# Attention scores on smaller tiles of the TensorE array: 32 queries by 96 keys in place of 64 by 128, with one kept PSUM tile, an earlier memset and a new written-out order

## The chip, the cores and the metric

The kernel runs on one core of one Trainium2 chip. The metric is the device time of one execution in microseconds (us), as the median of the runs. Beside it there is one profiled execution, with a record of each instruction; its span is the time from its first to its last instruction. The engines are called PE (TensorE: matrix products), DVE (VectorE), ACT (ScalarE), POOL (GpSimd) and SP (SyncE, which here only issues DMAs).

## The reference

Three layers follow one another, in float32. The first is attention over a sliding window of 64 positions; the second mixes each position with the one before it and runs a gated two-layer network; the third gates with a causal convolution of five taps.

```python
batch, n_heads, seq, head_dim = 4, 8, 576, 64        # attention
scores = scale * np.matmul(q, k.transpose(0, 1, 3, 2))
rel = pos[:, None] - pos[None, :]
mask = (rel >= 0) & (rel < 64)
scores = np.where(mask, scores, -1000000000.0)
attn = exp(scores - max);  attn = attn / (sum + 1e-09)
x = attn @ v                                          # -> (4, 576, 512)

xk = mu_k * x + (1.0 - mu_k) * x_prev                 # second layer
xr = mu_r * x + (1.0 - mu_r) * x_prev
k = np.maximum(xk @ w_k, 0.0)                         # 512 -> 1024
v = k * k @ w_v                                       # 1024 -> 512
x = sigmoid(xr @ w_r) * v

gate = sigmoid(sum of 5 taps of x)                    # third layer
out = gate * (x @ w_val) @ w_out
```

The weights come in as float64 and are put together from two 32-bit words on the chip.

## The kernel before

The 4 x 576 positions are cut into five blocks t: one of 256 and four of 512. Attention works on units u = (block t, pair of heads hp), four units to a block, 20 in all. A query sees the 63 keys before it and its own, so a unit cuts its positions into chunks of 64 queries, and a chunk meets 128 keys. Chunks sit in PSUM by twos: an even chunk on partitions 0 to 63, an odd one on 64 to 127, one PSUM bank for each of the two heads.

Each unit goes through a chain of steps: `ldqk` and `ldv` (DMAs that load q, k and v), `qk` (PE: the scores, line 425), `mask` and `edge` (DVE and POOL: scale the scores and take the minimum with a mask tile `cap`), `top` (DVE: row maximum), `exp` (ACT, line 469), `eps`, `rec`, `norm` (DVE: divide by the sum), `tp0` and `tp` (PE: transposes, line 487), `pt` (ACT or DVE: copy out of PSUM), `pv` (PE: times v, line 499) and `x` (copy out). In the units of blocks 0 and 1 (`BY_PE`) PE itself writes the mask: before the scores it multiplies an identity with the tile `low`, in bfloat16 (lines 417 and 421), and the scores are added onto that. The scores are float32; one such product of the program is two weight loads and two matrix passes in the trace, so that a unit of eight chunks and two heads has 32 records on PE.

Block 0 has its own PSUM pool of two score tiles (`p0`). From block 1 on each unit asks the pool `pq`, which has one buffer, for a new tile, which is free when the step that reads the scores (`exp` or `mask`) of the unit before is done.

The matrix products of the second layer are `h` (w_k), `r` (w_r) and `v` (w_v), 512 positions wide from block 1 on (line 590), and those of the third layer `val` and `out` (lines 859 and 965). They run on all 128 x 128 cells of the array; the scores run on 64 x 64 tiles of it, `pv` on 128 x 64.

The order of every step on every engine is fixed by a table, `SLOT`, which gives each step its place and, with a letter, its engine where there is a choice (`a` ACT, `v` DVE, `p` POOL). A small planner, `Plan`, walks through the steps in that order and emits them; it also holds a cost for each, and where its own clock shows PE free for longer than `WAIT`, the function `fill` puts in products of a zeroed 128 x 128 tile, `warm`, whose results nobody reads ("idle products", line 1144). It stops doing that once the first unit of block 1 has its scores. DMAs are issued by SP in the order of the table.

At the start POOL makes the mask (`cap`), then the identity (`ident`), and then zeroes `warm` (line 319); DVE derives `low` and `one` from the first two.

Of the kernel before, what the change touches and what calls it, by code (L numbers as in the profile page):

```python
# [8 lines left out]
F32 = mybir.dt.float32  # L9
# [11 lines left out]
P = 128  # L21
W = 64
NT = B * S
# [5 lines left out]
TB = 512  # L29
# [143 lines left out]
class Plan:  # L173
# [5 lines left out]
    WAIT, PASS = 700, 600  # L179
# [57 lines left out]
def tile_kernel(ctx, tc, qkh, vh, mu, conv, w_k, w_v, w_r, w_val, w_out, out):  # L237
# [55 lines left out]
    op = plan.op  # L293
# [906 lines left out]
```

## Time and profile before

| | before |
|---|---|
| median of 3 runs | 427.52 us (427.39 to 428.42) |
| the profiled execution's own time | 427.77 us |
| its span | 425.7 us |
| outside the span | 2.07 us |
| busy: PE, DVE, ACT, POOL | 97%, 82%, 62%, 6% of the span |
| mean granted clock of TensorE | 0.990 of 2.4 GHz |
| moved by DMA | 77.61 MB, mean 182 GB/s |

The table is of one execution, on the one core. Busy shares are means over stages with different limits, and the end of a matrix pass is modelled in the profile, so that passes that run side by side on several tiles overlap in it.

### The profile page before, as it was taken

How to read it: one execution, taken by the hardware profiler on the slowest of the kernel's cores; microseconds unless marked ns; L12 is line 12 of the kernel's file. 1: busy time of each engine (PE TensorE's matmuls, PEld its weight loads, DVE VectorE, ACT ScalarE, POOL GpSimd, SP SyncE). 2: the span in 40 equal slices, each digit the busy share in tenths (PEclk: the TensorE clock that was granted, in tenths of full speed). 3: DMA queues.
4: the chain of work that ended last, by engine and by line, in shares of the span. 5: the costliest groups of instructions: out<-in, count | busy, mean ns of one | idle time of the engine just before them, and what ended most of it. 6: DMA issues, size and time to landing. Idle time of an engine off the chain costs nothing.

```text
span 425.7 us, 7996 instructions
## 1 busy us (share of the span) xinstructions
PE 413.1 (97%) x3160; PEld 355.4 (83%) x3160; DVE 347.1 (82%) x506; ACT 264.0 (62%) x596; POOL 25.8 (6%) x66
## 2 busy tenths in 40 slices
PE   5799999999999999999999999999999999999996
PEld 4578888888888888888888888888888999999996
DVE  3889979989898786867597987697667799999970
ACT  4989998668869535867325776165331565668631
POOL 1101101010021000000000000000010000001000
PEclk9889999999999999999999999999999999999999
DMA  6999850553233444034039254177999940417623
GB/s 203 398 417 397 287 216 2 166 151 109 88 105 104 142 134 155 27 93 161 0 143 341 92 183 162 51 260 286 347 407 384 351 141 31 168 28 182 154 111 113
DMA packets 24709, 77.61 MB, mean 182 GB/s; under 512 B 2528, under 2 KB 3296, under 8 KB 22624
## 3 DMA queue, kind: packets, MB, share of 16 engines
q1 hardware_dynamic: 23088, 66.88, 44.5%
q0 software_dynamic: 1440, 10.22, 7.6%
q8 instruction: 25, 0.41, 0.4%
q14 instruction: 12, 0.10, 0.1%
q10 hardware_dynamic: 144, 0.00, 0.0%
HBM read 53.90 MB, written 20.84 MB: 176 GB/s over the span
## 4 chain that ended last, share of the span: by engine, by line
PE 80%; DVE 13%; ACT 2%; DMA 2%; issue 1%; POOL 0%; SPq 0%; ACTq 0%; POOLq 0%
PE h L590 21%; PE v L590 21%; PE r L590 10%; PE at L499 4%; PE at L487 4%; PE qk L425 4%; PE v L613 3%; PE out L965 3%; PE val0m L859 2%; DVE gq L757 2%; PE out2m L859 2%; DMA s<-w_v 2%; DVE x L757 2%; PE h L613 2%; PE r L613 2%; DVE xt L747 2%
## 5 line engine op out<-in xcount | busy, mean ns | idle before, releaser
L590 PE MATMUL h<-x,wk 128*128 128x512 f32 x384 | 91.4, 393 | 0.0
L590 PEld LDWEIGHTS h<-x,wk 128*128 128x128 f32 x384 | 71.2, 188 | 14.6
L590 PE MATMUL v<-sh,wv 128*128 128x512 f32 x256 | 81.7, 392 | 0.0
L590 PEld LDWEIGHTS v<-sh,wv 128*128 128x128 f32 x256 | 48.0, 188 | 9.9
L590 PE MATMUL v<-sl,wv 128*128 128x512 f32 x128 | 49.8, 389 | 0.0
L590 PE MATMUL r<-x,wr 128*128 128x512 f32 x192 | 45.8, 391 | 0.0
L469 ACT ACTIVATE s<-s,m 128x128 f32<-128x128 f32 x96 | 37.4, 396 | 13.1 <-DVE m L458 13.1
L790 DVE SCALAR_TENSOR_TENSOR early<-early,wc 128x576 f32<-128x576 f32 x48 | 38.3, 815 | 5.9 <-ACT early L788 5.3
L590 PEld LDWEIGHTS r<-x,wr 128*128 128x128 f32 x192 | 35.7, 188 | 7.3
L590 PEld LDWEIGHTS v<-sl,wv 128*128 128x128 f32 x128 | 24.1, 188 | 4.8
L670 DVE TENSOR_TENSOR sl<-rk,sh 128x1024 fp32r<-128x1024 f32 x16 | 19.6, 1222 | 8.6 <-ACT rk L668 8.5
L487 PE MATMUL at<-ident,s 128*128 128x128 f32 x144 | 23.9, 287 | 2.1 <-ACT xT L506 1.4
L499 PEld LDWEIGHTS at<-pt,vt 128*64 128x64 f32 x576 | 19.0, 140 | 7.7 <-issue 4.1
L550 DVE SCALAR_TENSOR_TENSOR xm<-xT,omu,xm 128x512 f32<-128x512 f32 x32 | 22.2, 748 | 3.1 <-POOL xT L556 1.6
L487 PEld LDWEIGHTS at<-ident,s 128*128 128x128 f32 x144 | 16.7, 142 | 8.0 <-ACT xT L506 2.3
L499 PE MATMUL at<-pt,vt 128*64 128x64 f32 x576 | 21.9, 228 | 1.2 <-DVE pt L493 1.2
L479 DVE TENSOR_TENSOR s<-s,m 128x1024 f32<-128x1024 f32 (+1 forms) x20 | 22.3, 1114 | 0.2
L425 PE MATMUL qk<-qk 64*64 64x128 f32 x576 | 22.1, 290 | 0.0
L640 ACT ACTIVATE rk<-h 128x512 f32<-128x512 f32 (+1 forms) x30 | 15.4, 535 | 10.2 <-PE h L590 9.2
L794 ACT ACTIVATE early<-early 128x1152 f32<-128x1152 f32 x6 | 7.0, 1170 | 21.9 <-DVE early L790 21.9
L573 DVE TENSOR_TENSOR x<-xm,x 128x1024 fp32r<-128x1024 f32 x16 | 19.2, 1219 | 1.6 <-ACT x L570 1.5
L469 ACT ACTIVATE s<-qk,m 128x128 f32<-128x128 f32 x48 | 16.9, 384 | 4.9 <-DVE m L461 4.9
(178 smaller groups left out, 845.8 us busy)
## 6 DMA issues: line engine op xcount, KB each, us to landing
qk<-qk SPq DMA_DIRECT2D x16, 544.0 KB, 5.6
vt<-vh SPq DMA_DIRECT2D x16, 512.0 KB, 4.8
xb<-x2d SPq DMA_DIRECT2D x4, 1152.0 KB, 7.1
out_t<-st SPq DMA_DIRECT2D x15, 288.0 KB, 2.4
x2d<-sgs SPq DMA_DIRECT2D x16, 256.0 KB, 4.9
w_out<-w SPq DMA_DIRECT2D x8, 512.0 KB, 2.9
w_val<-w SPq DMA_DIRECT2D x8, 448.0 KB, 3.1
wk<-w_val POOLq DMA_DIRECT2D x2, 1792.0 KB, 12.0
```

Source lines behind the costliest of these rows:

```text
L425: PE.matmul(a["ps"][heads[c % 2], h, c // 2 * P:c // 2 * P + P], lhsT=a["q"][heads[h], c * W:(c + 1) * W], rhs=a["k"][heads[h], c * W:c * ...
L469: ACT.activation(out=s, in_=scores()[:, c // n2, c % n2, :] if by_pe else s, func=AF.Exp, scale=D ** -0.5 if by_pe else 1.0, bias=l(0)[:, ...
L479: lambda: V.tensor_tensor(out=a["s"], in0=a["s"], in1=l(1).unsqueeze(2).to_broadcast(sq), op=ALU.mult))
L487: PE.transpose(a["tp", h][:, c * P:(c + 1) * P], a["s"][:, h * n2 + c, :], ident)
L499: PE.matmul(a["o"][heads[h], c * W:(c + 1) * W], lhsT=a["v"][:, c, heads[h]], rhs=a["pt"][:, h, c * W:(c + 1) * W], start=True, stop=True)
L550: V.scalar_tensor_tensor(out=m, in0=xT[:, f, :n], scalar=omu[:, c:c + 1], in1=m, op0=ALU.mult, op1=ALU.add)
L573: lambda E: E.tensor_tensor(out=dst(1), in0=src(), in1=f32(dst(0)), op=ALU.subtract))
L590: PE.matmul(ps, lhsT=a, rhs=b[:, kt, :], start=(kt == 0 and i == 0), stop=(kt == nk - 1 and i == 2))
L613: PE.matmul(Ps[key][:, :n], lhsT=ws(kt), rhs=x()[:, kt, :], start=kt == 0, stop=kt == nk - 1)
L670: lambda E: E.tensor_tensor(out=Ss[t][1][:, f, :n], in0=rk(), in1=f32(Ss[t][0][:, f, :n]), op=ALU.subtract))
L757: lambda E: E.tensor_tensor(out=lo(), in0=src(), in1=f32(hi()), op=ALU.subtract))
L790: V.scalar_tensor_tensor(out=o, in0=x, scalar=c, in1=o, op0=ALU.mult, op1=ALU.add)
```

## The change

The diff has four parts.

1. The scores: a chunk of 64 queries becomes two of 32, and each meets 96 keys (63 before its first query and its own 32, rounded up to whole halves of a chunk). Four such chunks stand beside each other on partitions 0, 32, 64 and 96, and with two heads the products are spread over eight tiles of 64 x 32 cells in place of four of 64 x 64. There are twice as many products, each 96 columns wide in place of 128. The 32 columns of each row that are no longer written hold what the tile held before, and the mask covers them.
2. The PSUM tile: from block 1 on all units write into one tile that is kept (`Q["scores"]`), the same one that the idle products write.
3. The start: the memset of `warm` is called ahead of `masks`, which now depends on it, and the planner may fill from 900 on its clock and reckons 430 for an idle product, where it had 1100 and 600.
4. The table `SLOT` and the planner's cost of `qk`. Nearly every number of the table differs; a line is shown.

```diff
 SLOT = {
-    'qk': '16 18 32 27 39 78 110 135 173 196 241 298 329 346 369 413 438 472 499 522',
+    'qk': '17 18 32 26 39 75 111 134 188 226 286 314 332 356 380 421 448 468 499 532',
...
+HW = W // 2
...
-    WAIT, PASS = 700, 600
+    WAIT, PASS, WARM = 700, 430, 900
...
-                self.fill(t, int((t - max(free.get("pe", 0), 1100) - 250) // self.PASS))
+                self.fill(t, int((t - max(free.get("pe", 0), self.WARM) - 250) // self.PASS))
...
+    warm = sgs[:, 0, :P]
+    op("warm", "pool", 110, [], lambda: G.memset(warm, 0.0))
+
     def masks():
...
-    op("cap", "pool", 1300, [], masks)
+    op("cap", "pool", 1300, ["warm"], masks)
...
         def qk():
-            a["ps"] = (pq if t else p0).tile([P, 2, TB], F32, tag="qk" if t else "p0", name=f"qk{u}")
+            a["ps"] = Q["scores"] if t else p0.tile([P, 2, TB], F32, tag="p0", name=f"qk{u}")
...
-            for c in range(nc_):
+            for c in range(2 * nc_):
+                rows = slice(c % 4 * HW, c % 4 * HW + HW)
                 for h in (0, 1):
-                    PE.matmul(a["ps"][heads[c % 2], h, c // 2 * P:c // 2 * P + P],
-                              lhsT=a["q"][heads[h], c * W:(c + 1) * W],
-                              rhs=a["k"][heads[h], c * W:c * W + P], start=not by_pe, stop=True,
+                    o = c // 4 * P + c % 2 * HW
+                    PE.matmul(a["ps"][rows, h, o:o + W + HW], lhsT=a["q"][heads[h], c * HW:(c + 1) * HW],
+                              rhs=a["k"][heads[h], c * HW:c * HW + W + HW], start=not by_pe, stop=True,
                               skip_group_check=by_pe)
-        op(("qk", u), "pe", 1034 * nc_ // 8 + ...
+        op(("qk", u), "pe", 822 * nc_ // 8 + ...
...
     def first_idle():
-        idle["ps"] = pq.tile([P, 2, TB], F32, tag="qk", name="idle")
+        idle["ps"] = Q["scores"] = pq.tile([P, 2, TB], F32, tag="qk", name="scores")
```

On POOL, at the very start of the program, this stood before (`cap` is the mask, `sgs` the tile whose first part is `warm`):

```order
L304 AFFINE_SELECT cap<-cap 64x128
L306 AFFINE_SELECT cap<-cap 64x128
masks.py:197 MEMSET ident 128x128
masks.py:199 AFFINE_SELECT ident<-ident 128x128
L319 MEMSET sgs 128x128
L297 MEMSET xT 128x4
```

This stands there after the change:

```order
L300 MEMSET sgs 128x128
masks.py:197 MEMSET ident 128x128
masks.py:199 ISA
masks.py:199 AFFINE_SELECT ident<-ident 128x128
L307 AFFINE_SELECT cap<-cap 64x128
L309 AFFINE_SELECT cap<-cap 64x128
```

The memset that the idle products wait for went from last but one to first, and the identity ahead of the mask.

On PE the program begins with the idle products and the first unit's mask and scores. Before:

```order
L1144 MATMUL idle<-sgs 128x128 x4
L417 LDWEIGHTS one
L417 MATMUL qk_159<-low,one 64x256
...
L417 MATMUL qk_159<-low,one 64x256
L425 MATMUL qk_159<-qk_122 64x128 x8
```

After:

```order
L1146 MATMUL scores<-sgs 128x128 x6
L418 LDWEIGHTS one
L418 MATMUL qk_161<-low,one 64x256
...
L418 MATMUL qk_161<-low,one 64x256
L428 MATMUL qk_161<-qk_123 32x96 x16
```

Six idle products stand there in place of four, and the unit's eight score products have become sixteen of 32 queries by 96 keys; the mask's own products keep their shape of 64 rows.

On SP, which issues the DMAs, the last pieces of w_v (line 355, 128x2048) stood between the loads of q, k and v for later units like this:

```order
L355 DMA words<-w_v 128x2048
L398 DMA qk_588<-qk 128x1088
L398 DMA qk_596<-qk 128x1088
L404 DMA vt_600<-vh 128x1024
L355 DMA words<-w_v 128x2048
L404 DMA vt_657<-vh 128x1024
L398 DMA qk_694<-qk 128x1088
L355 DMA x_118<-w_v 128x2048
L404 DMA vt_753<-vh 128x1024
L355 DMA s_119<-w_v 128x2048
```

After the change:

```order
L356 DMA words<-w_v 128x2048
L399 DMA qk_631<-qk 128x1088
L356 DMA words<-w_v 128x2048
L324 DMA cw<-conv 128x40
L405 DMA vt_720<-vh 128x1024
L356 DMA x_118<-w_v 128x2048
L399 DMA qk_732<-qk 128x1088
L356 DMA s_119<-w_v 128x2048
```

Between the first and the last piece of w_v there are now three loads of q, k and v where there were six.

## Rows read from the trace of the kernel before

**Rows 1.** Busy time of each engine by stretch, with instruction counts, granted clock and DMA.

```profile
core 0: us, PE busy (x) PEld busy (x) DVE busy (x) ACT busy (x) POOL busy (x), PEclk, DMA share, GB/s
5.00:10.00 5.00, 4.04 (x72) 3.33 (x71) 2.39 (x7) 2.28 (x13) 0.00 (x0) 1.00 0.61 179
15.00:20.00 5.00, 2.78 (x34) 1.80 (x38) 4.00 (x10) 4.88 (x22) 0.73 (x1) 0.77 1.03 390
20.00:25.00 5.00, 5.00 (x57) 4.08 (x50) 4.79 (x10) 3.43 (x8) 0.00 (x0) 0.55 1.03 419
25.00:60.00 35.00, 35.00 (x441) 29.34 (x439) 31.32 (x43) 34.05 (x104) 4.39 (x8) 1.00 0.90 340
70.00:164.00 94.00, 94.00 (x935) 77.42 (x935) 84.04 (x114) 66.12 (x195) 8.15 (x23) 1.00 0.36 113
328.00:421.00 93.00, 91.69 (x680) 90.59 (x679) 80.77 (x116) 54.50 (x84) 3.88 (x7) 1.00 0.47 146
```

**Rows 2.** Score passes (line 425) by short stretch: in brackets, passes under way in it.

```profile
153.71:153.74 0.03, 0.02 (x4) 1.00 0.00 0
153.74:153.87 0.13, 0.13 (x4) 1.00 0.00 0
153.87:153.90 0.03, 0.03 (x8) 1.00 0.00 0
153.98:154.01 0.03, 0.03 (x12) 1.00 0.00 0
```

**Rows 3.** Chain that ended last, around that unit: start, length, what.

```profile
152.71 1.08 PE at L499 x32
153.79 1.03 PE qk L425 x32
```

**Rows 4.** The score passes as a group: count, busy us, mean ns, idle before.

```profile
L425 PE MATMUL qk<-qk 64*64 64x128 f32 x576 | 22.1, 290 | 0.0
```

**Rows 5.** PE in order of time, a unit whose mask PE writes.

```profile
35.29 0.41 PE L417 MATMUL qk<-low,one 64*64 64x512 bf16 x4
35.53 0.27 PE L425 MATMUL qk<-qk 64*64 64x128 f32 x2
```

**Rows 6.** The same chain as in Rows 3, its first 20 us.

```profile
3.05 0.15 POOL sgs L319
...
3.25 2.08 PE idle L1144 x8
...
7.72 0.99 ACT s L469 x5
...
18.60 0.69 PE at L487 x2
```

**Rows 7.** SP, POOL and DVE at the start, in order of time.

```profile
0.74 1.80 SPq L398 DMA_DIRECT2D qk<-qk  x4
...
1.07 0.29 POOL L304 TENSOR_SCALAR_AFFINE_SELECT cap<-cap 64x128 f32<-64x128 f32 x1 [0.63 <-DVE cap L300]
...
2.48 0.20 POOL masks.py:197 MEMSET ident<- 128x128 f32 x1
...
3.08 0.23 DVE L315 CAST one<-ident 128x128 bf16<-128x128 f32 x1 [0.32 <-POOL ident masks.py:199]
```

**Rows 8.** The tile `qk`, first 12 us: its DMAs from issue to landing.

```profile
DMA to landing us min/median/max: 3.0/3.8/5.9
```

**Rows 9.** The same chain as in Rows 3, from 50 us to 61 us.

```profile
50.31 8.22 DMA s<-w_v
...
58.55 0.70 DVE s L340
...
60.44 0.66 PE at L487 x4
```

**Rows 10.** Waits of PE: its line, whom it waited for, us, times, longest.

```profile
PE val3m L859 <- DVE early L900: 0.7, 1, 0.7
PE out2m L859 <- ACT x L754: 0.6, 1, 0.6
```

More of the change, by code (lines that the diff above doesn't have):

```diff
@@ L316, in tile_kernel @@
     op("low", "dve", 700, ["cap", "ident"], lows)
-    warm = sgs[:, 0, :P]
-    op("warm", "pool", 110, [], lambda: G.memset(warm, 0.0))
     op("table", "act", 100, ["warm"], lambda: ACT.activation(out=sgs[:, 1, :1], in_=warm[:, :1], func=AF.Exp), table="exp")
@@ L422, in qk @@
                                           rhs=low[heads[h], P:], start=False, stop=True, skip_group_check=True)
-            for c in range(nc_):
+            for c in range(2 * nc_):
+                rows = slice(c % 4 * HW, c % 4 * HW + HW)
                 for h in (0, 1):
-                    PE.matmul(a["ps"][heads[c % 2], h, c // 2 * P:c // 2 * P + P],
-                              lhsT=a["q"][heads[h], c * W:(c + 1) * W],
-                              rhs=a["k"][heads[h], c * W:c * W + P], start=not by_pe, stop=True,
+                    o = c // 4 * P + c % 2 * HW
+                    PE.matmul(a["ps"][rows, h, o:o + W + HW], lhsT=a["q"][heads[h], c * HW:(c + 1) * HW],
+                              rhs=a["k"][heads[h], c * HW:c * HW + W + HW], start=not by_pe, stop=True,
                               skip_group_check=by_pe)
-        op(("qk", u), "pe", 1034 * nc_ // 8 + (208 if t == 0 else 241) * by_pe, [("ldqk", u), *(["low"] if by_pe else []), *([] if t else ["idle"])], qk,
+        op(("qk", u), "pe", 822 * nc_ // 8 + (208 if t == 0 else 241) * by_pe, [("ldqk", u), *(["low"] if by_pe else []), *([] if t else ["idle"])], qk,
            ring=("pq" if t else "p0", ("exp" if by_pe else "mask", u)))
```

247 rows, old and new, of the table SLOT are left out of this document.

## The prediction

> **What bounds the kernel now.** I read the busy times by stretch first [rows 1]. From 25 us on PE is busy all the time: 35.00 us of 35, later 94.00 of 94, and 91.69 of 93 in the last stage. A busy PE need not be a fast one, so I looked at how the passes follow each other, and then at the chain that ended last, which lies almost wholly on PE from 19 us on. Time that PE saves after 25 us is therefore time saved at the end, as long as what PE needs also comes earlier. ACT leaves it little room in 25 to 60 us: it is busy for 34.05 of 35 us [rows 1]. Before 19 us PE waits for others: the chain runs from a POOL memset over idle products to the first scores, and then along ACT's exponentials, which begin at 7.72, until PE takes over at 18.60 [rows 6].
>
> The scores themselves are bound by their tiles. In one unit four passes are under way within the first 0.03 us, none joins them until 153.87, then four more come within 0.03 us, and again four from 153.98 on [rows 2]. Four tiles work side by side, all four are refilled at once, and a steady round takes 153.98 - 153.87 = 0.11 us: 1.03 us for a unit [rows 3] is 8 rounds (32 passes on 4 tiles) of 0.11 = 0.88, and a rest of 0.15. The rest is a longer first round (153.87 - 153.71 = 0.16 for 0.11) and the changes of the array's shape on the way in and out. No score pass waited for anything [rows 4].
>
> **The scores of blocks 2 to 4.** Removed are 32 passes on four tiles, added 64 on eight: again 8 rounds, each over 96 columns in place of 128. I scale the round with its columns: 0.11 x 96/128 = 0.083. A unit saves 8 x 0.027 = 0.22 us and takes 0.81, if the rest of 0.15 stays. Twelve units of blocks 2 to 4 lie in the stretches where PE never pauses [rows 1]: **-2.6 us**. No row shows 64x32 tiles, so this has bounds: nothing saved if the rest grows by what the rounds lose, and the loss in the first rival. The weight loads double in number, but each has half the columns and they run beside the passes as now. The kept PSUM tile costs nothing: a unit had to wait for the reader of the unit before it already, since the pool had one buffer, and that wait is covered by the `pv` and h, r, v products between two units [rows 4]. Without that cover PE would stand for the reader's time.
>
> **The scores of blocks 0 and 1.** Here the mask's passes come first, on 64x64 tiles. Now the scores follow 0.24 us after the mask's start, while a 512-column pass of the mask still shows as under way [rows 5]: the shape stays. After the change it changes between the two, eight times. The price lies between 0 and the whole rest of 0.15 us; I take 0.10, the part of it that is not the longer first round. The four units of block 1 then save 0.22 - 0.10 each, 0.5 together, and since ACT has only 0.95 us to spare there I count **-0.3 us** (bounds -0.9 and 0). The four half units of block 0 save 0.11 and pay 0.10. The Trainium skill (TensorEngine Tiling (Array Packing), Key Properties) says that a change of tiling mode, as against a change of tile, drains the engine; by it nothing near -0.9 can come of this term, and with the whole 0.15 for a drain it would be 4 x 0.07 = -0.3.
>
> **The start.** The idle products began at 3.25, right behind the memset at 3.05 [rows 6]. POOL could take up its own work at about 1 us: the first mask step at 1.07 had waited for DVE [rows 7]. With the memset in front I put the first idle product at 1.2. Four of them, 8 passes, took 2.08 us [rows 6], 0.26 a pass; six take 3.1, so that the mask's passes can begin at 4.3 and not at 5.33. Two other things must be there: q and k, issued at 0.74 and landing 3.0 us later, at 3.7 [rows 7, 8]; and `low` and `one`, for which POOL now works through memset (0.15), identity (2.48 to 3.05: 0.57) and mask (1.07 to 2.48: 1.41) from 1.0 to 3.1, and DVE another half microsecond, to some 3.7 [rows 6, 7]. So the first scores and ACT's exponentials come 1.0 us earlier, and what follows to 19 us hangs on ACT: **-1.0 us**. Bounds: 0, if the DMAs decide (their share is 1.03 from 15 to 25 us [rows 1]); -2.1, the memset's whole lead. In 5 to 10 us the DMA share was 0.61, partly since the next loads wait for the first scores, so loads can move up too.
>
> **The new order.** PE waited 1.3 us in the last stage (93.00 - 91.69 [rows 1]), nearly all of it twice [rows 10]. Another order can remove that or add as much: -1.3 to +1.3, and I take **0**. The places where PE changes its shape are the same but for one or two, by the order, 0.1 us each.
>
> **The sum.** -2.6 - 0.3 - 1.0 = -3.9: a span of 421.8 after 425.7, with the 2.07 us outside it 423.9. The profiled execution took 427.77, 0.25 above the median of 427.52, so the median to expect is **423.6 us**.
>
> **Rivals.**
>
> *PE can't start passes fast enough (slower).* A pass begins on average every 0.11/4 = 0.0275 us, and `pv`, on two tiles, is no faster: 32 passes in 1.08 us [rows 3]. If this is what PE can issue and not what the tiles take, 64 passes need 1.76 us and a unit 1.91, 0.88 more than now; with 16 full and 4 half units, 18 x 0.88 = 15.8, less 1.0 at the start: 442. The change loses in the scores as soon as a round of eight takes over 0.11, a start each 0.014 us. Against it: four passes begin within 0.03 us and then none for 0.13 [rows 2]; PE waits for tiles. But nowhere do more than four begin at once. I give it 0.12. The Trainium skill (TensorE: Matmul & The Clock Gate, section "Wait — 56ns, not 53.3ns?") states that start-to-start never drops below about 25 ns however small the product; by that a unit would take 64 x 0.025 + 0.15 = 1.75 and the kernel 439.5 (18 x 0.72 less 1.0). The rows speak against the rule as it stands, with four starts in 30 ns.
>
> *The clock no longer falls.* It was at 0.77 on average from 15 to 20 us and 0.55 from 20 to 25 [rows 1], that is at 1.2 GHz from about 17.7 to 24.5, after a stretch in which PE was busy for 2.78 us of 5. The same 5.0 busy us of 20 to 25 at full clock need 2.75: 2.2 us less, 421.4. More idle products (six and four for four and two in the order) speak for it; that they end in both kernels with block 1's first unit, long before 15 us, against it: 0.12.
>
> *The DMAs hold the start's gain back.* The last piece of w_v, issued at 50.31, landed at 58.55; DVE waited for it, and PE's transposes at 60.44 for DVE [rows 9]. If it lands no earlier, the 1.3 us gained before it are lost there: 424.9. Three loads fewer stand ahead of it now, against this: 0.12.
>
> *The scores gain nothing.* The rest grows by 0.22 with eight tiles; only the start is left: 426.5. 0.07.
>
> *The new order stalls.* It would need 3.9 us of new waits to eat the gain, three times those of the last stage [rows 10]; 427.5 to 430: 0.05.
>
> **How the numbers follow.** The forecast has the rest, 0.52, with a range of its own of 422.4 to 425.0. About 0.3% (1.3 us) is what a measurement of this kernel can tell from no change: faster is below 426.2, slower above 428.8. Faster: 0.52 + 0.12 + 0.12 = 0.76. The fourth rival and half of the fifth are no change: 0.09. The first and the other half are slower: 0.15. From 421.0 to 427.0 leaves out the first rival, most of the fifth and the edge of the second, 0.2.
>
> **What would show it.** A unit's 64 passes in 0.81 us on the chain, eight starts within some 0.05 us and a round of 0.08; passes at an even spacing of 25 ns or more would show the first rival. In blocks 0 and 1 a gap of about 0.1 us between mask and scores. The first exponential near 6.7 us. PE without a pause from 24 us on; the clock in 15 to 25 us; the landing of the last w_v before 58 us. I am wrong if a unit takes over 1 us, or if PE waits more than 1.3 us in the last stage.

## The result, and the profile after

The changed kernel is slower: 431.19 us median of 8 runs (430.0 to 433.84), against 427.63 us for the kernel before on the same chip (8 runs), a ratio of 1.0084 [1.0058, 1.0109]. The forecast was 423.6. The profiled execution took 432.7 us, with a span of 430.9 in place of 425.7.

First the view by stretch, which answers to [rows 1]: busy time of each engine with instruction counts, granted clock, DMA share.

```profile
core 0: us, PE busy (x) PEld busy (x) DVE busy (x) ACT busy (x) POOL busy (x), PEclk, DMA share, GB/s
15.00:20.00 5.00, 4.39 (x92) 3.00 (x94) 4.08 (x11) 4.90 (x20) 0.58 (x1) 0.54 1.00 399
20.00:25.00 5.00, 5.00 (x46) 4.04 (x47) 4.69 (x7) 3.53 (x19) 0.00 (x0) 0.77 1.03 419
25.00:60.00 35.00, 35.00 (x505) 29.78 (x504) 33.65 (x44) 34.17 (x85) 1.76 (x6) 1.00 0.87 330
70.00:164.00 94.00, 94.00 (x1287) 77.16 (x1286) 80.75 (x110) 69.93 (x201) 4.35 (x22) 1.00 0.38 121
320.00:330.00 10.00, 4.15 (x19) 3.19 (x17) 9.93 (x16) 3.07 (x4) 0.11 (x1) 0.97 0.32 124
330.00:340.00 10.00, 8.84 (x49) 8.85 (x50) 6.56 (x10) 1.30 (x2) 0.43 (x1) 0.69 1.00 352
```

Up to 320 us PE is as full as before. Then it is busy for 4.15 us of 10, and afterwards its clock is granted at 0.69 on average. The waits of PE (whom it waited for, us, times, longest) show one new entry for the last stage, where [rows 10] had nothing over 0.7:

```profile
PE val0m L861 <- DVE x L759: 7.0, 1, 7.0
...
PE val3m L861 <- DVE x L759: 0.3, 1, 0.3
```

`val0m` is the third layer's first product. Its group in the view by lines (count, ns of one as min/median/max, first and last start) gives the start of that layer; first after, then before:

```profile
L861 PE MATMUL val0m<-x,wk x84: 290/295/608, 323.9 to 346.1; 128*128 128x288 f32 x84
```

```profile
L859 PE MATMUL val0m<-x,wk x84: 292/295/302, 327.9 to 340.6; 128*128 128x288 f32 x84
```

So the changed kernel was 4.0 us ahead when the third layer began. From there to the end it took 430.9 - 323.9 = 107.0 us in place of 425.7 - 327.9 = 97.8. Of these 9.2 us the wait is 7.0, and the halved clock behind it makes up about the rest: one product takes up to 608 ns, and on the chain 59 passes take 10.41 us where 60 took 7.99 before, 2.4 more. That piece of the chain before:

```profile
328.09 7.99 PE val0m L859 x60
```

The chain after tells where the 7 us come from (start, length, what):

```profile
299.29 0.37 SPq L798
299.66 0.05 issue
299.88 19.01 DMA xb<-x2d
...
319.01 0.76 DVE xt L749
...
331.16 10.41 PE val0m L861 x59
```

The load of `xb`, the x of the third layer, is under way for 19.01 us. DVE then works through the last taps and the preparation of x until 331, ahead of PE. The timeline of POOL and SP's queue shows which other loads went out then:

```profile
290.79 1.27 POOL L1117 DMA_DIRECT2D wk<-w_val  x2 [90.66 <-PE h L592]
302.33 0.53 POOL L1120 DMA_DIRECT2D wr<-w_out  x1 [9.50 <-PE r L592]
302.85 1.07 POOL L1120 DMA_DIRECT2D wol<-w_out  x2
303.89 0.57 POOL L1120 DMA_DIRECT2D wr<-w_out  x1
```

```profile
295.25 0.37 SPq L779 DMA_DIRECT2D early<-x2d  x1
299.29 0.37 SPq L798 DMA_DIRECT2D gd<-early  x1
299.88 0.62 SPq L724 DMA_DIRECT2D xb<-x2d  x1
300.55 1.24 SPq L808 DMA_DIRECT2D gate<-gd  x1
```

And the same before, first on POOL, then the load of `xb` on SP's queue:

```profile
297.81 0.71 POOL L1115 DMA_DIRECT2D wk<-w_val  x1 [2.67 <-PE h L590]
302.57 0.55 POOL L1118 DMA_DIRECT2D wol<-w_out  x1 [4.05 <-DVE sl L670]
309.12 1.06 POOL L1118 DMA_DIRECT2D wr<-w_out  x2 [6.00 <-PE r L590]
310.17 0.55 POOL L1115 DMA_DIRECT2D wk<-w_val  x1
```

```profile
294.82 0.62 SPq L722 DMA_DIRECT2D xb<-x2d  x1
```

The DMA page gives 1792 KB for each `wk` load and 1024 KB for each of the four others, 7.7 MB together; at the 361 to 408 GB/s that the stretch from 300 to 320 us moves, that is about 20 us of all DMA engines, an estimate. Before, one `wk` went out at 297.81 and the other at 310.17, and `xb` stood ahead of both (issued at 294.82, 5.9 us to land). Now both go out at 290.79 and 291.49, ahead of everything that the third layer's start needs. They don't delay it alone: by the profile both had landed by 304.6 us (7.6 and 13.1 us after their issue), and `xb` was under way for another 14 us, beside the four loads of w_out that went out behind it.

The scores (chain, one unit, to compare with [rows 3]) did get shorter, by less than forecast (the chain runs through 55 of the unit's 64 passes):

```profile
149.93 0.93 PE scores L428 x55
```

### The profile page after: what moved, and what is told of

Read it like the earlier page. It is cut to its first block, busy times and chain, and to the rows that moved or that the text cites. A ratio compares the mean times of both kernels' runs of the same rounds, so it can differ in the third digit from the quotient of the medians.

```text
span 430.9 us, 9154 instructions
## 1 busy us (share of the span) xinstructions
PE 415.3 (96%) x3744; PEld 356.5 (83%) x3744; DVE 355.4 (82%) x524; ACT 253.5 (59%) x579; POOL 19.2 (4%) x67
## 4 chain that ended last, share of the span: by engine, by line
PE 72%; DVE 19%; DMA 6%; issue 1%; ACT 1%; SPq 0%; ACTq 0%; POOL 0%; DVEq 0%; POOLq 0%
PE h L592 18%; PE v L592 15%; PE r L592 8%; DMA xb<-x2d 4%; PE at L501 4%; PE at L489 4%; PE scores L428 4%; DVE x L759 4%; PE v L615 3%; PE h L615 3%; PE out L967 3%; PE val0m L861 2%; PE out2m L861 2%; DVE early L792 2%; DVE gq L759 2%; DVE xt L749 2%
## 5 line engine op out<-in xcount | busy, mean ns | idle before, releaser
L592 PE MATMUL v<-sh,wv 128*128 128x512 f32 x256 | 82.7, 394 | 0.0
L792 DVE SCALAR_TENSOR_TENSOR early<-early,wc 128x576 f32<-128x576 f32 x48 | 38.6, 813 | 11.3 <-ACT early L790 11.1
L642 ACT ACTIVATE rk<-h 128x512 f32<-128x512 f32 (+1 forms) x25 | 12.8, 541 | 13.6 <-PE h L592 8.7
L861 PE MATMUL val0m<-x,wk 128*128 128x288 f32 x84 | 14.1, 333 | 7.0 <-DVE x L759 7.0
L756 ACT ACTIVATE x<-xt 128x576 fp32r<-128x576 f32 x15 | 10.1, 681 | 18.1 <-issue 11.5
L861 PEld LDWEIGHTS val0m<-x,wk 128*128 128x128 f32 x84 | 13.6, 224 | 7.4 <-DVE x L759 7.3
```

The source lines that it names most:

```text
L592: PE.matmul(ps, lhsT=a, rhs=b[:, kt, :], start=(kt == 0 and i == 0), stop=(kt == nk - 1 and i == 2))
L792: V.scalar_tensor_tensor(out=o, in0=x, scalar=c, in1=o, op0=ALU.mult, op1=ALU.add)
L861: PE.matmul(z[bank][:, j, :HS], lhsT=lhs, rhs=rhs, start=new and kt == 0 and e == 0, stop=kt == 1 and e == 2, skip_group_check=not new)
```

## Experiments

All ratios are to the kernel before on the same chip; us of change are the ratio less 1, times 427.5.

| kernel | median us | ratio [95%] | change |
|---|---|---|---|
| e1: new scores only | 425.92 | 0.9973 [0.9958, 0.9988] | -1.2 |
| e4: new start only | 425.81 | 0.9967 [0.9950, 0.9984] | -1.4 |
| e8: both, old order | 425.81 | 0.9958 [0.9935, 0.9981] | -1.8 |
| e2: changed kernel, old scores | 434.98 | 1.0183 [1.0158, 1.0209] | +7.8 |
| e3: changed, `xb` load ahead | 433.06 | 1.0123 [1.0092, 1.0154] | +5.3 |
| e5: changed, w_val loads later | 426.72 | 0.9959 [0.9941, 0.9977] | -1.8 |
| e6: e5 and e3 | 425.99 | 0.9947 [0.9919, 0.9975] | -2.3 |
| e11: before, w_val loads together | 434.58 | 1.0185 [1.0166, 1.0205] | +7.9 |
| e9: changed, third layer's old order | 424.17 | 0.9930 [0.9909, 0.9951] | -3.0 |
| e10: e9 with old scores | 425.48 | 0.9964 [0.9948, 0.9980] | -1.5 |

**The parts apart (e1, e4, e2, e8).** e1 is the kernel before with the new score function and the kept tile alone; e4 has only the start:

```diff
-    'cap': '4',
+    'cap': '9',
-    'warm': '10',
+    'warm': '2',
-    WAIT, PASS = 700, 600
+    WAIT, PASS, WARM = 700, 430, 900
-    op("cap", "pool", 1300, [], masks)
+    op("cap", "pool", 1300, ["warm"], masks)
```

e2 is the changed kernel with the old score function, e8 the sum of e1 and e4. What was expected of e1:

> The kernel before with the scores alone changed (32 queries by 96 keys on eight tiles, the kept PSUM tile); start and order are those of before. In the profile of the changed kernel a unit of scores in blocks 2 to 4 took 0.93 us where it took 1.03, and a unit of block 1 with its mask 1.30 where it took 1.27. If that is all, 12 x -0.10 + 4 x 0.03 = -1.1 us: 426.5. Theory 'the order is to blame': 426 to 427. Rival 'the scores themselves lose time somewhere': 428 or more.

Of e4:

> The kernel before with the start alone changed: memset first, then identity and mask, six and four idle products in place of four and two; scores and order of before. In the changed kernel the third unit of block 1 began its mask at 26.92 and not 28.89, 2.0 us earlier. Theory 'the start's gain reaches the end': 425.5 to 426. Rival 'the last piece of w_v, landing at 58.55, holds it back': 427 to 427.5, with a longer wait of PE at 60 us.

Of e2:

> The changed kernel with the scores of before (64 by 128 on four tiles, a new PSUM tile for each unit); its start and its order stay. Theory 'the order is to blame': PE comes to the third layer 1.1 us later and waits there for the same late data, 6 us in place of 7, so the time stays near 431 (430 to 433). Rival 'the scores themselves lose': back to 427 or below.

Of e8:

> The kernel before with its order, plus the new start and the new scores with the kept tile. Theory: the two parts add up: -1.4 for the scores and -1.5 for the start as each alone gave, 424.4 us (423.9 to 425.0), and then the new order alone is worth about +6.8 us. Rival (the parts are held back by the same DMA, the last pieces of w_v, or by ACT's exponentials): no better than either alone, 425.8 us.

Each part alone gains, and of these kernels and the changed one only the two with the new order lose: e2, with the old scores, is even slower than the changed kernel and than the 430 to 433 expected. PE waits 9.4 us for `x` there, and `xb` is under way for 21.35 us. So neither the scores nor the start cause the loss. e8 doesn't tell whether the two gains add up: its median is where the rival had it, but its interval reaches from -0.8 to -2.8 us and holds the sum of -2.6 too. In e8's profile, its slowest execution, one transfer of w_r is under way for 9.82 us on the chain in the first 20 us; the runs of one kernel here differ by 1 to 6 us.

**The load of xb (e3).** The first theory was that `xb` is late because it stands behind the gate's store on SP's queue:

```diff
-    'ldx': '893 943 958 1015',
+    'ldx': '877 943 958 1015',
```

> The changed kernel with one number of its table altered: the load of the third layer's first batch (step ldx 0) moves ahead of the last-but-one gate's load and store on SP, behind the weight stores. Theory 'that load is late since it stands behind a store that waits for DVE and ACT': it is issued near 291 and not 299.9, lands by 300 and not 318.9, PE's wait of 7.0 us ahead of the third layer and the slow clock after it (2.3 us) go: 422 to 423. Rival 'DVE's backlog ahead of the third layer makes the data late in any case': the wait stays over 4 us, 428 or more. Rival 'the transfer is slow, since it shares the DMA engines with the other loads': issue earlier, landing still after 312.

The theory fell. `xb` now landed 14 us earlier, and PE still waited 6.7 us; on the chain another transfer of the same time had taken its place:

```profile
298.49 16.21 DMA gd<-early
...
314.81 0.79 ACT early L790
```

Of the two, the one that stands second on SP's queue is the one that lands late: in the changed kernel the store, issued at 299.29, landed in 7.5 us and `xb` behind it in 19.01. DVE takes the taps of the early gate (L792) ahead of x's preparation (L749 to L759), and stands until the store's buffer is free.

**The loads of w_val (e5, e6).** The next theory: the two `wk` loads fill the DMA engines.

```diff
-    'wv2': '870 872',
+    'wv2': '899 901',
```

> The changed kernel, with the two large loads of w_val moved on POOL's queue behind the first load of w_r (issued after about 301 us and not at 290.79 and 291.49). Theory: the 7 us wait of PE at the start of the last stage comes from these two loads, which fill the DMA engines while the x of the gate's early taps, its store and its reload stand in line. Then xb lands by about 306 us in place of 318.9, the wait is under 1 us, the clock does not fall at 330 us, and the time is 422 to 424 us. Rival (DVE's queue of taps and x preparation is late by itself, or the loads of w_r and w_out do the same): the wait stays above 5 us and the time at 428 us or more. A smaller loss is possible if w_val now lands after 324 us and PE waits for it instead.

> The changed kernel with both edits: the two loads of w_val later, and the load of xb ahead of the gate's store. Theory (full DMA engines): 421.5 to 423.5 us, no wait above 1 us at the start of the last stage, xb landing by about 301 us; little or no better than the later loads alone, since xb is then no longer last. Rival (DVE's queue or the other loads): 428 us or more, as the xb load moved by itself gave.

This line alone takes back 5.3 us (1.0084 to 0.9959). Two lines of POOL's timeline of e5, and PE's waits there:

```profile
305.34 0.71 POOL L1120 DMA_DIRECT2D wr<-w_out  x1 [9.42 <-PE r L592]
306.04 0.57 POOL L1117 DMA_DIRECT2D wk<-w_val  x1
```

```profile
PE val1m L861 <- DVE gate L907: 1.5, 1, 1.5
...
PE val0m L861 <- DVE early L902: 0.8, 1, 0.8
```

The 7 us wait and the fall of the clock behind it are gone. `xb` now goes out ahead of all six loads and lands in 6.2 us, though the six follow each other within 3 us (SP's queue in e5):

```profile
302.87 0.61 SPq L724 DMA_DIRECT2D xb<-x2d  x1
```

But the medians of both kernels lie 2.7 and 2.5 us above the ranges expected, and two smaller waits are there. On the chain of e6 stands the second load of `xb`, issued as the last block's values come in:

```profile
322.56 9.19 DMA xb<-x2d
...
331.77 0.77 DVE xt L749
```

Before, this load took 6.9 us: it went out at 328.12, and the last of the six landed at 328.2. In e6 the last of them lands at 325.7, 3 us after this load went out. That the six loads make it late is likely by these times, but no run takes it apart.

From the first `val0m` to the end e6 needs 421.8 - 322.4 = 99.4 us, 1.6 more than before.

**Two loads together in the old order (e11).** If the loads do the harm, the kernel before should lose by them too:

```diff
-    'wv2': '906 878',
+    'wv2': '879 878',
```

> The kernel before, with its second large load of w_val put right behind the first on POOL's queue (both from about 297.8 us, in place of 297.81 and 310.17). Theory (the loads do harm only where they stand ahead of the early gate's load, its store and the load of xb, and here xb is issued at 294.8): xb lands by 303 us, no wait over 1.5 us at the start of the last stage, 427 to 428.5 us. Rival (the two loads one behind the other do it wherever they stand): a wait of 3 us or more and 430 us or more.

My theory, that they harm only where they stand ahead of `xb`, fell, and the rival's numbers came. `xb` landed in 5.9 us, yet the kernel lost 7.9 us: the gate's store, which goes out behind the two loads, took 15.71 us, where it took 6.8 us before (chain of e11):

```profile
305.91 15.71 DMA gd<-early
...
321.73 0.78 ACT early L788
322.50 0.49 ACT sgs L680
...
323.04 10.02 PE v L590 x36
```

ACT's step L788 waits for that store, the copy L680 stands behind it on ACT, and PE waited 3.7 us for the copy in the middle of the second layer. That is about half of the loss. The clock, granted at 0.79 and 0.86 on average from 320 to 325 and from 325 to 330 us, comes on top: the third layer begins at 332.9 us, 5.0 later than before. It then takes 432.6 - 332.9 = 99.7 us in place of 97.8. So it is not one transfer that has to be put ahead: whichever transfer of a waiting chain goes out behind the two loads can be the late one. That they follow each other is not enough for the harm, as e5 shows, where they do so behind those transfers.

**The old third layer (e9, e10).** e9 is the changed kernel with the steps of the third layer at the places that `SLOT` gave them before (`wv2`, `wo2`, `ldx`, `ldg`, `val`, `out`, the steps between and the last steps of the early gate, renumbered to fit; all other steps keep their order; its lines stand 11 lower than the changed kernel's):

```diff
-    'wv2': '870 872',
+    'wv2': '907 878',
-    'wo2': '898 904 900 902',
+    'wo2': '899 904 912 894',
-    'ldx': '893 943 958 1015',
+    'ldx': '871 946 957 1016',
...
```

> The changed kernel with its new scores and start and its new order up to the third layer, but the third layer's steps (its loads of w_val and w_out, of x and of the gate, products, copies and stores) at the places that they had before. Theory (all that the new order loses, it loses in the third layer: first by the loads of w_val, then by some 2 us of waits for DVE that stayed when these were moved): from the first val product to the end about 97.9 us, as before, in place of 107.1 and of 99.4 to 99.9 with the loads moved; 424 to 425 us. Rival (the old third layer doesn't fit the new second layer, and new waits come): 426 us or more.

> The same with the old scores on 64x64 tiles and the pool's tile. Theory (a unit of blocks 2 to 4 gains 0.10 us, twelve of them 1.2): 1 to 1.5 us above the kernel with the old third layer and the new scores, 425.2 to 426.5 us. Rival (what the scores gain is held back elsewhere once the start is early): no difference, within 0.4 us.

Both came as the theories had it. e9 has the lowest ratio of all, though its interval meets those of e6 and e8; it is below the kernel before (424.17 to 426.76 us) and 1.5% below the changed one by their ratios. Its third layer begins at 325.5 and ends at 423.5, 98.0 us, as before:

```profile
L850 PE MATMUL val0m<-x,wk x84: 288/295/302, 325.5 to 338.2; 128*128 128x288 f32 x84
```

e10 is 1.3 us above e9: the scores keep their gain behind the early start. And e10, with the new start and the new order of the first two layers, gains what e4 gains with the start alone (-1.5 and -1.4): up to the third layer the new order is worth nothing that these runs can tell.

**What a score pass costs (e7).** e1 with each pass cut to 32 of its 96 key columns, so that the scores against the other 64 keys are left out. It is one execution, read for its trace alone:

```diff
-                    PE.matmul(a["ps"][rows, h, o:o + W + HW], lhsT=a["q"][heads[h], c * HW:(c + 1) * HW],
-                              rhs=a["k"][heads[h], c * HW:c * HW + W + HW], start=not by_pe, stop=True,
+                    PE.matmul(a["ps"][rows, h, o:o + HW], lhsT=a["q"][heads[h], c * HW:(c + 1) * HW],
+                              rhs=a["k"][heads[h], c * HW:c * HW + HW], start=not by_pe, stop=True,
```

> The kernel before with the new scores and the kept tile, each score pass cut from 96 to 32 key columns (the scores against 64 of a chunk's 96 keys are left out). Theory (PE's instruction feed sets a unit's time once some 32 passes have begun): a unit of blocks 2 to 4 still takes 0.80 to 0.93 us, with passes beginning at an even spacing of about 0.0167 us. Rival (tiles bind, a round goes with its columns): a round of 0.03 to 0.04 us and a unit of 0.35 to 0.5 us.

The unit took 0.69 us, between the two. Score passes by stretch, each from just ahead of a unit's first pass, so that the number in the first brackets counts the passes begun; first the changed kernel, then e7:

```profile
149.80:149.91 0.11, 0.05 (x8) 0.06 (x12) 1.00 0.05 21
...
149.80:150.19 0.39, 0.33 (x32) 0.34 (x33) 1.00 0.03 12
...
149.80:150.62 0.82, 0.76 (x64) 0.77 (x64) 1.00 0.01 6
```

```profile
151.43:151.66 0.23, 0.18 (x32) 0.18 (x33) 1.00 0.00 0
...
151.43:152.06 0.63, 0.58 (x64) 0.58 (x64) 1.00 0.00 0
```

The busy time is that since the first pass. The first 32 passes begin within 0.33 us, or 0.18 with a third of the columns: there the columns count. The second 32 need 0.76 - 0.33 = 0.43 us, and 0.58 - 0.18 = 0.40 with a third of the columns: there they hardly do, and each start takes 0.40/32 = 0.0125 us on average.

## Why the prediction was wrong, step by step

**The step that failed: "The new order".** I took 0, with bounds of 1.3 us either way from the waits that PE had before. The runs put it at +6.6 us, all of it in the third layer (1.0084 for the changed kernel and 0.9930 for e9, which differ in that alone): `xb` landed in 19.0 us and not 5.9, and PE stood for 7.0 us. The parts then are -1.4 (e4), -1.2 (e1) and +6.6: +4.0, where +3.6 was measured. The bounds were the error: the old waits say how well the old order fits, and nothing of how badly another one can. The order of POOL's queue, with both `wk` loads in a row and early where they had stood 12 us apart, was there to be read beforehand in the two tables; I looked at SP's order at the start only. The rival "The new order stalls" named the right mechanism, and its time of 427.5 to 430 was too low, since it had no place and no transfer in it. That the place of the `wk` loads is the cause is shown by e5 and e11 from both sides, for 5.3 of the 6.6 us; where in the third layer's order the other 1.3 lie is open. That the fall of the clock adds 2.4 us to the wait is read from the changed kernel's rows alone.

**"The scores of blocks 2 to 4": right in kind, mis-sized.** A unit was to take 0.81 us and takes 0.93, so that twelve gain 12 x 0.10 = 1.2 in place of 2.6; e1 measured 1.2, and e9 against e10 1.3. Eight passes begin within 0.05 us, and the first four rounds take the forecast 0.08 each (0.33 for 32). The scaling failed in the second half of a unit, where a start takes at least 0.0125 us and a round of eight thus 0.10 or more.

**"PE can't start passes fast enough".** This rival was wrong by its number, 0.0275 us a start, and right in kind for half of a unit: 0.0125 is just under the 0.014 from which the change was to lose in the scores. The rule of the Trainium skill that it stood beside (TensorE: Matmul & The Clock Gate, section "Wait — 56ns, not 53.3ns?"), about 25 ns from start to start, would by estimate make a unit's 64 starts 1.6 us long; the 0.76 us measured speak against it for products on different tiles.

**"The scores of blocks 0 and 1": -0.3 forecast, no gain seen.** One unit of block 1 with its mask took 0.34 + 0.02 + 0.01 + 0.90 = 1.27 us on the chain before, and takes 1.30 now:

```profile
26.99 0.34 PE scores L418 x4
27.34 0.03 PE scores L422 x2
27.36 0.93 PE scores L428 x56
```

The 0.10 that a unit of blocks 2 to 4 gains is gone here. The timeline shows the gap that was to be expected: the first score pass begins 0.38 us after the mask's start, where it was 0.24 [rows 5], 0.14 later.

```profile
26.92 0.41 PE L418 MATMUL scores<-low,one 64*64 64x512 bf16 x4
27.17 0.20 PE L422 MATMUL scores<-low,one 64*64 64x64 bf16 x2
27.30 0.31 PE L428 MATMUL scores<-qk 64*32 64x96 f32 x8
```

So the change between 64x64 and 64x32 tiles comes to some 0.14 where I took 0.10, and the term, 4 x 0.03 = +0.1 us, lies at the edge of its bounds of 0 and -0.9.

**"The start": -1.0 forecast, -1.4 measured (e4).** The first idle product begins at 0.99 and not at 1.2, and the first exponential at 6.26 us where it was 7.72, 1.5 earlier and not 1.0. PE has no pause from 24 us on up to 323.9, as forecast, and w_v holds nothing back, so "The DMAs hold the start's gain back" didn't come true at that place; in e4, with the old order, the last w_v landed at 57.0 us and not 58.55. "The clock no longer falls" didn't either in the changed kernel: 0.54 and 0.77 from 15 to 25 us.

**The condition named for being wrong** was a unit over 1 us or over 1.3 us of waits of PE in the last stage. The second came true.

Open are what changes after 32 passes of a unit (the starts themselves or the weight load that each pass has; no run takes the two apart), and whether the gains of start and scores add up in full in the old order.

## What to carry to other kernels

When a table of numbers reorders a program, list every large load that has moved and ask which transfers of a waiting chain now go out behind it: 7.7 MB of weights fill the DMA engines for about 20 us here (the estimate above) wherever they stand, and what decides is who waits for a transfer that goes out in that time. Bound a new order by what it could delay (the DMA engines' backlog), not by the waits of the old one. To find a culprit among many moved steps, put back one stage's places at a time: one line of the table returned 5.3 us here, and the old third layer under the new first two gave the kernel with the lowest time.

## What the runs showed of the hardware

A load or store that took 5.9 or 6.8 us before took 15.7 to 21.4 us when it was issued 8 to 9 us behind two loads of 1792 KB on another engine's queue (the changed kernel, e2, e3, e11); the store that stood just ahead of the late load on its own queue landed in 7.5. Starts of score passes on eight tiles came 8 in 0.05 us at first and 0.0125 us apart on average after 32 passes. And the clock's fall at the start is not fixed by the program: the changed kernel, e3, e5 and e6 differ only in steps from about 290 us on, and from 15 to 20 us their clocks were granted at 0.54, 0.66, 0.64 and 1.00. The stretch in e6:

```profile
15.00:25.00 10.00, 8.14 (x136) 6.23 (x133) 9.42 (x18) 9.39 (x39) 0.99 (x2) 1.00 1.01 404
```

PE was busy for 8.14 us of these 10 at full clock; in the changed kernel it was 9.39 of 10, with about as many passes (92 and 46), partly at half. What decides between the two, no run here shows.
